# Loads of a two-part activation in the second stage: the low parts issued from ScalarE's queue instead of SyncE's

## The chip, the core and the metric

The kernel is one program on one core of a Trainium2 chip. The metric is the device time of one execution in microseconds (us), the median of several runs. The core's engines are named as in the profile: PE (TensorE matmuls), PEld (its weight loads), DVE (VectorE), ACT (ScalarE), POOL (GpSimd) and SP (SyncE). SPq and ACTq are DMA issues by SP and by ACT.

## The reference, cut to what matters

Three layers run one after the other over 8 batches of 576 tokens: attention with pooled keys and values, a gated MLP with a spatial mixing matrix, and a layer of four small attention experts of which each token takes two. The diff touches only the third, whose input x is the second layer's output:

```python
logits = x @ w_gate                                  # best 2 of 4 experts, softmax weights w
for e in range(4):
    q, k, v = x @ wq[e], x @ wk[e], x @ wv[e]        # x: 576 x 512, head width 64
    scores = causal(0.125 * (q @ k.transpose(0, 2, 1)))
    a = softmax(scores)
    ye = a @ v @ wo[e]
    out += w_e * ye                                  # for tokens that chose e
```

## The kernel before

The program has two stages. The first (class PhaseA) computes the attention and the MLP of all 8 batches, ends near 585 us in the trace, and leaves x in DRAM as two fp32r parts that add up to the fp32 value: a high part and a low part (line 466). The second (class PhaseB) is the expert layer. Each matmul product of it is made of three passes, high by high, low by high and high by low.

**Loading x.** For each batch, load_x is called four times, once for each chunk kc of 128 of the 512 features. Each call issues three DMAs from SP: the high part (line 642, tile xbh, 288 KB), the low part (line 643, into xbl, 288 KB) and a copy of the last 64 tokens of the low part beside the high one (line 644, 32 KB). There is one tile xbl for all four chunks and no second copy: the loads of the next batch wait until the last projection of this batch has read it.

**Units.** A batch is 18 units: two pairs p of experts with 9 units u each. Unit u=0 is the 64 tokens left over of both experts at once, u=1 to 4 are 128 tokens of the first expert with 512, 384, 256 and 128 keys, u=5 to 8 the same of the second. For one unit PE makes the scores (line 839 or 827, tile s), DVE takes the maximum (line 841), ACT the exponential (line 844, tile pr), DVE sum and reciprocal (lines 855, 856), POOL or DVE scales (line 860), PE transposes (line 886 or 873, tile t), and ACT and DVE copy the transposed block as high and low part (lines 890, 891; for u=0 lines 877, 882). The transposes run three units behind the scores (LAG = 3). After u=5 and u=8, PE multiplies by the values (line 906, tile av): ACT and DVE add its two halves (lines 910, 911) and split the sum (lines 916, 917), and the output projection (lines 928 to 931) reads that.

**Filling in.** Between the units stand other pieces of work, by the table FILL: in pair 0 the projections of pair 1 ('12 10 11' and '13', lines 713 to 715, copied by lines 726 to 745), then the loads of the next batch ('x0 x1 x2 x3') straight behind '13', then the output projections of the batch before ('o3 o1 o0'); in pair 1 the value and pair-0 projections of the next batch ('v0', 'v1 00 02', ...). The first batch has its own table without the output projections, the last one loads nothing.

**What sets the order.** Instructions are recorded in the order of the code. When the program is built, a scheduler orders each engine's queue by its own estimate of when operands are there, and each engine then runs its queue strictly in that order. All PSUM tiles of the second stage share eight banks, so a matmul that starts a new tile waits until the readers of the bank's last tile are done. The DMAs of SP and ACT share eight completion counters (DMAHW0 to DMAHW7), which are handed out in turn: an issue waits until the DMA that used its counter eight DMAs ago has landed.

Of the kernel before, what the change touches and what calls it, by code (L numbers as in the profile page):

```python
# [8 lines left out]
F32 = mybir.dt.float32  # L9
# [615 lines left out]
class PhaseB:  # L625
# [8 lines left out]
    def load_x(self, b, kc):  # L634
        nc, w = self.nc, self.w
        if kc == 0:
            self.X[b] = []
            self.xlt = w.tile([128, 4, S], F32R, tag="qt", name="xbl")
        xh = w.tile([128, 640], F32R, tag="P", name="xbh", bufs=5)
        xl = self.xlt[:, kc]  # L640
        d = self.x2d[b][:, kc]
        nc.sync.dma_start(xh[:, :S].bitcast(F32), d[:, 0])
        nc.sync.dma_start(xl.bitcast(F32), d[:, 1])
        nc.sync.dma_start(xh[:, S:].bitcast(F32), d[:, 1, 512:])
        self.X[b].append((xh, xl))

# [369 lines left out]
```

## Time and profile before

| | us |
|---|---|
| runs before: median (lowest to highest) | 962.95 (962.15 to 963.11) |
| the profiled execution | 959.79 |
| its span, first to last instruction | 958.0 |
| PE / DVE / ACT / POOL busy in the span | 909.0 / 688.1 / 518.0 / 445.8 |

The profile is of one execution, whose own time lies 3.2 us under the median of the runs and 1.8 us over its span. The mean granted TensorE clock is 0.983 of full speed.

### The profile page before, as it was taken

The page shows a single profiled execution, that of the slowest core. Times are in us where ns is not written, and L with a number is a line of the kernel's source. Part 1 is how long each engine was busy: PE and PEld are TensorE (multiplying, and loading weights), DVE is VectorE, ACT ScalarE, POOL GpSimd, SP SyncE. Part 2 cuts the span into 40 slices and gives each one's busy share as a digit, 9 for nine tenths or more (in the row PEclk, how much of TensorE's full clock was granted, in tenths as well). Part 3 has the DMA queues.
Part 4 walks back from the last instruction along what each step waited for, and adds up shares of the span by engine and source line. Part 5 has one row for each costly group of instructions (what it writes and reads, how often), then busy time and mean ns, then how long its engine had stood idle before and what let it go on. Part 6 is the DMA issues. An engine that isn't in the chain of part 4 may idle for free.

```text
span 958.0 us, 18445 instructions
## 1 busy us (share of the span) xinstructions
PE 909.0 (95%) x6488; PEld 862.2 (90%) x6488; DVE 688.1 (72%) x1869; ACT 518.0 (54%) x1285; POOL 445.8 (47%) x628
## 2 busy tenths in 40 slices
PE   4887699999999999999999999899999999999997
PEld 3676689989989999899899899799999999999987
DVE  6998458757667577587576524897879797878785
ACT  3765344343443343443443433677777776877776
POOL 6545847558369377475583461122222222323221
PEclk9798899999999999999999999999999999999999
DMA  9611422312402403223116014415353534435121
GB/s 323 244 35 44 162 92 83 122 61 72 160 23 87 156 24 132 99 83 121 62 50 206 13 41 133 141 37 178 79 172 87 160 98 134 133 95 165 49 62 75
DMA packets 51644, 102.86 MB, mean 107 GB/s; under 512 B 10592, under 2 KB 16736, under 8 KB 50656
## 3 DMA queue, kind: packets, MB, share of 16 engines
q1 hardware_dynamic: 51408, 101.68, 33.0%
q8 instruction: 52, 0.85, 0.4%
q14 instruction: 40, 0.33, 0.1%
q10 hardware_dynamic: 144, 0.00, 0.0%
HBM read 59.72 MB, written 28.31 MB: 92 GB/s over the span
## 4 chain that ended last, share of the span: by engine, by line
PE 77%; DVE 11%; ACT 4%; POOL 3%; issue 2%; DMA 2%; SPq 1%; POOLq 0%; ACTq 0%; DVEq 0%
PE av L906 4%; PE op L457 4%; PE op L458 4%; PE op L459 3%; PE sc L224 3%; PE up L416 3%; PE up L418 3%; PE sp L434 3%; PE sp L433 3%; PE sp L432 3%; PE up L417 3%; PE vp L355 3%; PE vp L356 3%; PE vp L357 3%; PE t L886 3%; PE pj L715 2%
## 5 line engine op out<-in xcount | busy, mean ns | idle before, releaser
L860 POOL TENSOR_SCALAR pr<-pr,sm,gw 128x128 f32<-128x128 f32 (+3 forms) x119 | 72.2, 609 | 208.4 <-DVE sm L856 137.6
L844 ACT ACTIVATE pr<-s,sm 128x256 f32<-128x256 f32 (+4 forms) x160 | 83.0, 520 | 41.9 <-DVE sm L841 18.0
L458 PE MATMUL op<-g,woh 128*128 128x288 f32 x256 | 76.9, 301 | 8.0 <-POOL g L445 8.0
L432 PE MATMUL sp<-wsh,vnh 128*128 128x288 f32 x256 | 78.2, 307 | 5.3 <-ACT vnh L400 5.3
L416 PE MATMUL up<-x,wih 128*128 128x288 f32 x256 | 76.9, 300 | 1.6 <-ACT xu L324 1.6
L457 PE MATMUL op<-g,woh 128*128 128x288 f32 x256 | 77.5, 307 | 0.3 <-DVE x2l L464 0.3
L433 PE MATMUL sp<-wsh,vnl 128*128 128x288 f32 x256 | 76.7, 300 | 0.4 <-DVE vnl L402 0.3
L434 PE MATMUL sp<-wsl,vnh 128*128 128x288 f32 x256 | 76.3, 298 | 0.0
L418 PE MATMUL up<-x,wil 128*128 128x288 f32 x256 | 75.8, 296 | 0.0
L715 PE MATMUL pj<-xbh,wql 128*128 128x288 f32 x256 | 75.5, 295 | 0.0
L714 PE MATMUL pj<-xbl,wqh 128*128 128x288 f32 x256 | 75.5, 295 | 0.0
L713 PE MATMUL pj<-xbh,wqh 128*128 128x288 f32 x256 | 75.4, 295 | 0.0
L459 PE MATMUL op<-g,wol 128*128 128x288 f32 x256 | 75.4, 299 | 0.0
L417 PE MATMUL up<-x,wih 128*128 128x288 f32 x256 | 75.1, 293 | 0.0
L841 DVE CUSTOM_DVE_ANT_0 s<-s,mk 128x512 f32<-128x512 f32 (+3 forms) x128 | 62.4, 487 | 3.5 <-PE t L886 2.9
L891 DVE TENSOR_TENSOR pbl<-t,pbh 128x512 fp32r<-128x512 f32 (+3 forms) x128 | 60.7, 484 | 3.3 <-ACT pbh L890 1.7
L886 PE MATMUL t<-ident,pr 128*128 128x128 f32 x320 | 57.7, 280 | 4.8 <-POOL pr L860 2.6
L224 PE MATMUL sc<-kbd,qt 128*128 128x144 f32 (+1 forms) x320 | 49.8, 303 | 11.5 <-DMA qt<-q_in 8.9
L906 PE MATMUL av<-pbh,vt 128*128 128x320 f32 (+4 forms) x224 | 55.7, 278 | 2.4 <-ACT pbh L890 2.4
L400 ACT ACTIVATE vnh<-vg,rs 128x512 fp32r<-128x512 f32 (+1 forms) x40 | 27.3, 718 | 54.9 <-POOL rs L392 43.0
L224 PEld LDWEIGHTS sc<-kbd,qt 128*128 128x128 f32 (+1 forms) x320 | 44.3, 191 | 14.0 <-issue 11.4
L458 PEld LDWEIGHTS op<-g,woh 128*128 128x128 f32 x256 | 48.7, 190 | 8.4 <-POOL g L445 8.2
(247 smaller groups left out, 3305.3 us busy)
## 6 DMA issues: line engine op xcount, KB each, us to landing
kraw<-k_in SPq DMA_DIRECT2D x16, 576.0 KB, 3.8
x<-x2h SPq DMA_DIRECT2D x32, 288.0 KB, 2.1
x<-x2l SPq DMA_DIRECT2D x32, 288.0 KB, 2.1
xbl<-x SPq DMA_DIRECT2D x32, 288.0 KB, 4.0
xbh<-x SPq DMA_DIRECT2D x32, 288.0 KB, 3.8
kd<-scr SPq DMA_DIRECT2D x64, 144.0 KB, 2.5
out<-o SPq DMA_DIRECT2D x32, 288.0 KB, 3.4
vraw<-v_in SPq DMA_DIRECT2D x16, 512.0 KB, 4.2
```

The source lines that it names most:

```text
L224: nc.tensor.matmul(ps[:m, p // 2, (p % 2) * 144:(p % 2) * 144 + 144], qt[:, p, o:o + m], kbd[:, p, :], start=p % 2 == 0, stop=True, skip_g ...
L416: nc.tensor.matmul(o, self.wi[0][:, kc, c], xh, start=kc == 0, stop=False)
L417: nc.tensor.matmul(o, self.wi[0][:, kc, c], xl, start=False, stop=False)
L418: self.upmm = nc.tensor.matmul(o, self.wi[1][:, kc, c], xh, start=False, stop=kc == 3).ins
L432: nc.tensor.matmul(o, vh[:, k, c], self.ws[0][:, k, s], start=k == 0, stop=False)
L433: nc.tensor.matmul(o, vl[:, k, c], self.ws[0][:, k, s], start=False, stop=False)
L434: nc.tensor.matmul(o, vh[:, k, c], self.ws[1][:, k, s], start=False, stop=False)
L457: nc.tensor.matmul(o, self.wo[0][:, k, c], gh[:, s], start=k == 0, stop=False)
L458: nc.tensor.matmul(o, self.wo[0][:, k, c], gl[:, s], start=False, stop=False)
L459: nc.tensor.matmul(o, self.wo[1][:, k, c], gh[:, s], start=False, stop=k == 3)
L715: nc.tensor.matmul(ps, self.wq[1][:, kc, c], xh[:, s], start=False, stop=kc == 3)
L906: nc.tensor.matmul(ps[:, s - lo:], vt[:, j, 2 * p + e].rearrange("p a d -> p (a d)"), t[:, e, j * PTS + s:j * PTS + up], start=j == 0 and ...
```

## The change

The 32 loads of the low parts (four for each batch) are issued by ACT; the 64 others of load_x stay on SP. Tiles, sizes, and the arithmetic are as they were.

```diff
@@ PhaseB.load_x
         nc.sync.dma_start(xh[:, :S].bitcast(F32), d[:, 0])
-        nc.sync.dma_start(xl.bitcast(F32), d[:, 1])
+        nc.scalar.dma_start(xl.bitcast(F32), d[:, 1])
         nc.sync.dma_start(xh[:, S:].bitcast(F32), d[:, 1, 512:])
```

Since the scheduler orders all queues anew, the order moves on other engines too. Two places follow, both in the third batch of the second stage, in pair 0, just behind the projection '13'. The loads there are those of the fourth batch (x_3).

ACT's queue before, from the last copies of the q projection (734) to the exponential of unit 4 (844, 128x128):

```order
L734 ACTIVATE qs_6011<-pj 64x64
L744 ACTIVATE scr<-pj 128x288 [waits PE_49]
L844 ACTIVATE pr,sm<-s,sm 128x256 [waits DVE_49]
L910 ACTIVATE scr<-av 64x256 [waits PE_49]
L916 ACTIVATE ah<-scr 128x256 [waits DVE_49]
L910 ACTIVATE scr<-av 64x320 [waits PE_49]
L877 ACTIVATE pbh<-t_7743 128x4x2x64 [waits PE_49,Activation_49]
L877 ACTIVATE pbh<-t_7750 64x2x64 [waits PE_49]
L916 ACTIVATE ah<-scr 128x320 [waits DVE_49]
L844 ACTIVATE pr,sm<-s,sm 128x128 [waits DVE_49]
```

and ACT's queue after, over the same stretch (the names in brackets are the counters waited for):

```order
L734 ACTIVATE qs_6011<-pj 64x64
L643 DMA xbl<-x_3_60 128x576 [waits DMAHW1_49,DMAHW0_49,PE_49]
L844 ACTIVATE pr,sm<-s,sm 128x256 [waits DVE_49]
L744 ACTIVATE scr<-pj 128x288 [waits PE_49]
L643 DMA xbl<-x_3_60 128x576
L643 DMA xbl<-x_3_60 128x576 [waits DMAHW6_49]
L643 DMA xbl<-x_3_60 128x576 [waits DMAHW0_49]
L910 ACTIVATE scr<-av 64x256 [waits PE_49]
L910 ACTIVATE scr<-av 64x320 [waits PE_49]
L877 ACTIVATE pbh<-t_7743 128x4x2x64 [waits PE_49,Activation_49]
L877 ACTIVATE pbh<-t_7750 64x2x64 [waits PE_49]
L844 ACTIVATE pr,sm<-s,sm 128x128 [waits DVE_49]
```

The four issues stand in it, three of them in a row ahead of the first copy of av (910), the last one waits for counter 0 (the one of the high-part load of chunk 1, which SP issues a little earlier), and both 916 have moved behind the exponential of unit 4.

DVE's queue before, from the first sum of av's halves (911) to the maximum of unit 5 (841, 128x512):

```order
L911 TENSOR_TENSOR scr<-av,scr 64x256
L917 TENSOR_TENSOR al<-scr,ah 128x256
L911 TENSOR_TENSOR scr<-av,scr 64x320
L841 ISA s,sm<-s,mk 128x128
L841 ISA sm 128x1
L882 TENSOR_TENSOR pbl<-t_7743,pbh 128x4x2x64
L917 TENSOR_TENSOR al<-scr,ah 128x320
L882 TENSOR_TENSOR pbh<-t_7750,pbh 64x2x64
L891 TENSOR_TENSOR pbl<-t,pbh 128x4x128
L841 ISA s,sm<-s,mk 128x512
```

and DVE's queue after:

```order
L745 TENSOR_TENSOR qs_6011<-pj,scr 128x288
L841 ISA s,sm<-s,mk 128x128
L841 ISA sm 128x1
L841 ISA s,sm<-s,mk 128x512
L841 ISA sm 128x1
L911 TENSOR_TENSOR scr<-av,scr 64x256
L911 TENSOR_TENSOR scr<-av,scr 64x320
L882 TENSOR_TENSOR pbl<-t_7743,pbh 128x4x2x64
L917 TENSOR_TENSOR al<-scr,ah 128x256
L917 TENSOR_TENSOR al<-scr,ah 128x320
```

The maxima of units 4 and 5 (841, 128x128 and 128x512) have moved ahead of the two sums 911. On PE the order here stays as it was up to the output projection: scores of unit 5, transposes of unit 2, scores of unit 6 (839, 128x384), then 928; only a few matmuls of 928 to 930 change places among themselves. In both programs the scores of unit 6 take the bank of av's first half and wait for 911 64x256.

The same two pictures stand in six batches, the second to the seventh. In the first batch the three issues stand ahead of the copies 877 instead (there is no output projection), and the eighth loads nothing.

## Rows read from the trace of the kernel before

**Rows 1.** Page, part 1: busy us, share of the span, instructions.
```profile
PE 909.0 (95%) x6488; PEld 862.2 (90%) x6488; DVE 688.1 (72%) x1869; ACT 518.0 (54%) x1285; POOL 445.8 (47%) x628
```

**Rows 2.** Windows: length, busy us by engine, granted clock, DMA share, GB/s.
```profile
600.00:650.00 50.00, 45.43 (x332) 43.14 (x331) 43.03 (x176) 34.34 (x110) 9.57 (x16) 0.97 0.37 102
650.00:800.00 150.00, 149.49 (x1156) 146.71 (x1155) 120.69 (x483) 112.49 (x355) 40.38 (x64) 1.00 0.44 132
```

**Rows 3.** Timeline of PE: start, us, instruction, [idle before <- releaser].
```profile
651.34 0.42 PE L839 MATMUL s<-kd,qs 128*128 128x384 f32 x1
...
695.76 0.39 PE L840 MATMUL s<-qs,qzvlo 128*128 128x512 f32 x1
...
696.24 0.42 PE L839 MATMUL s<-kd,qs 128*128 128x384 f32 x1
696.49 0.34 PE L840 MATMUL s<-qs,qzvlo 128*128 128x384 f32 x1
696.67 0.28 PE L928 MATMUL op<-ah,wqh 128*128 128x256 f32 x1
...
876.28 0.42 PE L839 MATMUL s<-kd,qs 128*128 128x384 f32 x1
```

**Rows 4.** Timeline of DVE, third batch of the second stage.
```profile
694.53 0.42 DVE L911 TENSOR_TENSOR scr<-av,scr 64x256 f32<-64x256 f32 x1
...
695.89 0.48 DVE L911 TENSOR_TENSOR scr<-av,scr 64x320 f32<-64x320 f32 x1
696.30 0.28 DVE L841 CUSTOM_DVE_ANT_0 s<-s,mk 128x128 f32<-128x128 f32 x1
...
698.64 0.69 DVE L841 CUSTOM_DVE_ANT_0 s<-s,mk 128x512 f32<-128x512 f32 x1
```

**Rows 5.** Timeline of ACT, the same place.
```profile
692.48 0.45 ACT L734 ACTIVATE qs<-pj 64x64 fp32r<-64x64 f32 x2 [0.36 <-DVE qs L731]
692.95 0.41 ACT L744 ACTIVATE scr<-pj 128x288 fp32r<-128x288 f32 x1
693.53 0.47 ACT L844 ACTIVATE pr<-s,sm 128x256 f32<-128x256 f32 x1 [0.17 <-DVE sm L855]
...
694.12 0.38 ACT L910 ACTIVATE scr<-av 64x256 f32<-64x256 f32 x1
...
696.79 0.35 ACT L844 ACTIVATE pr<-s,sm 128x128 f32<-128x128 f32 x1
```

**Rows 6.** All issues of line 643: ns min/median/max, and us from issue to landing.
```profile
L643 SPq DMA_DIRECT2D xbl<-x x32: 325/430/1244, 503.3 to 879.0; - x32
...
DMA to landing us min/median/max: 2.9/4.0/5.5
```

**Rows 7.** The only DMA issued by ACT (line 83).
```profile
L83 ACTq DMA_DIRECT2D cm<-cm_in x1: 409/409/409, 0.7 to 0.7; - x1
```

**Rows 8.** Timeline of SP: at the program's start, and in the third batch.
```profile
0.74 0.86 SPq L58 DMA_DIRECT2D kraw<-k_in  x2
...
691.64 0.54 SPq L642 DMA_DIRECT2D xbh<-x  x1
```

**Rows 9.** Timeline of PE, ACT: first batch of the second stage.
```profile
604.97 0.75 ACT L877 ACTIVATE pbh<-t 128x512 fp32r<-128x512 f32 x2
...
612.18 1.09 PE L886 MATMUL t<-ident,pr 128*128 128x128 f32 x4 [1.45 <-DVE sm L855]
```

**Rows 10.** Windows, columns as in Rows 2: first batch, last batch.
```profile
611.00:612.00 1.00, 0.00 (x0) 0.00 (x0) 1.00 (x6) 0.77 (x3) 0.00 (x0) 0.95 0.97 321
612.00:613.00 1.00, 0.82 (x5) 0.85 (x5) 0.79 (x8) 0.23 (x2) 0.43 (x1) 0.50 1.03 336
...
614.00:615.00 1.00, 1.00 (x7) 1.00 (x6) 0.88 (x2) 0.25 (x2) 0.00 (x0) 0.50 0.78 275
...
945.00:949.00 4.00, 3.13 (x23) 2.88 (x23) 2.62 (x8) 2.21 (x7) 0.00 (x0) 1.00 0.07 24
```

**Rows 11.** Timeline of ACT at the last scores of the first stage.
```profile
505.03 0.69 ACT L245 ACTIVATE e<-e 64x576 f32<-64x576 f32 x1 [1.37 <-DVE e L237]
```

## The prediction, written before the changed kernel was run

> **What bounds the kernel now.** Read first the page's busy shares [rows 1]: PE is busy 95% of the span, no other engine above 72%. Such a share is a mean, so the windows come next. In the second stage's steady part PE is busy 149.49 of 150 us at full clock, ACT 112.5 and DVE 120.7; only around the first batch, from 600 to 650 us, is PE idle for 4.6 us [rows 2]. So from the second batch on whatever makes PE wait is paid in full, there is next to nothing for earlier loads to win (0.5 us in 150), and a wait that is inserted once per batch counts as often as it stands. Last comes the timeline of each engine at the place where the loads stand. I walk the third batch: PE runs the scores of unit 5 to 696.15 (695.76 + 0.39), starts those of unit 6 (128x384) at 696.24 and the output projection at 696.67 with no idle time before any of these; the unit-6 scores stand at 651.34 in the first of six alike batches and at 876.28 in the last [rows 3].
>
> **The change part by part.**
>
> *What SP loses.* Four issues of 0.43 us per batch [rows 6], 1.7 us of a queue that PE does not wait for. Gain: none, by the 0.5 us just read; bound at 0.5 us.
>
> *What ACT gets.* The same 32 issues. I price one at 0.43 us; the one DMA that ACT issues today took 0.41 [rows 7]. In total 32 x 0.43 = 13.8 us on an engine that idles 37.5 us in 150 [rows 2]. The mean would hide it; the place decides. Walk ACT's new queue on the old clock [rows 5]: the copies of line 734 end at 692.93; the first 643 runs to 693.4 and fits into the 0.17 us of idle time and the slot that 744 had; the exponential of unit 3 goes from 693.53 to 694.1; 744 (0.41) to 694.5. Three issues follow. The last one also waits for its counter, that is for the high part of chunk 1 to land, issued at 691.64 [rows 8]; with 4.0 us for a load of this size [rows 6] that is 695.64, about when it comes up anyway (694.5 + 2 x 0.43 = 695.4). It ends at 696.1. Then 910 (0.38) to 696.5 instead of 694.5, the second 910 to 696.9, the two 877 to 697.6, and the exponential of unit 4 with its readout to 698.1, where it began at 696.79.
>
> *What DVE's new order does.* The maxima of units 4 and 5 now precede both sums 911. The maximum of unit 5 cannot begin before PE has ended that unit's scores at 696.15, and it holds DVE about 0.7 us [rows 3, 4]. So 911 64x256 starts near 696.9 and ends near 697.3; before it ran from 694.53 to 694.95 [rows 4]. In both programs PE's scores of unit 6 wait for just this sum, since they take its bank: they start at about 697.35 instead of 696.24, 1.1 us late. This does not hang on what a DMA issue costs on ACT: its copy 910 is done at 696.5, 0.4 us before DVE is free for the sum.
>
> *What is late next.* After the unit-6 scores PE would reach the output projection at about 697.8 (0.43 us behind, as in 696.24 to 696.67). Its first bank is now the one of unit 4's scores, freed by ACT's exponential at 698.1. So it starts 1.4 us late (698.1 against 696.67). Behind it nothing gives time back: PE waits for nothing later in the batch, so it carries the 1.4 us on. The copies 916 and splits 917 come about when PE asks for them; I count nothing for them.
>
> *Bounds per batch.* Below, 1.1 us: issues on ACT cost nothing and only DVE's order counts. Above: the landing takes its maximum of 5.5 us [rows 6], the last issue begins at 697.1 instead of 695.64, and the projection starts 2.9 us late. I take 1.4, because 4.0 is the median and ACT's own 0.41 is the nearest row to its issue.
>
> *The first batch.* Same four issues, other table: they stand ahead of the two 877 (604.97 before [rows 9]), which go about 2.4 us later (one issue and 744 ahead of them more or less in free time, the rest not). PE is starved there anyway, so part is absorbed: between 0 and 2.4, I take 1.0, since the wait that ends the starved stretch (1.45 us for DVE [rows 9]) is at the end of the same chain.
>
> *The four loads of the first batch,* issued in the first stage: ACT idles 1.37 us before its next exponential there [rows 11], so two issues (0.86) are hidden and the others stand in front of a copy with idle time around it. Nothing; at most 0.9 us once if the cover were gone.
>
> *Other queues.* The counters tie SP to ACT: the third kd copy of pair 1's keys now waits for ACT's first load to land (about 697). Keys are needed only when pair 1 begins, behind all output projections; nothing, but up to 1.5 us per batch if landings stretch to 5.5. Loads of chunk 3 come no later than before, since SP has fewer issues ahead of them.
>
> *Sum.* 6 x 1.4 + 1.0 = 9.4 us. On the profiled execution that makes 959.79 + 9.4 = 969.2; its time lies 3.2 below the median of the runs, on which it makes 962.95 + 9.4 = **972.3 us**, 1.0% slower.
>
> **A rule weighed against this.** The rows first: ACT's one issue took 0.41 us at 0.7 us, while SP issued two in 0.86 [rows 7, 8], so one pair in which both queues issue at once shows no surcharge. The Trainium skill, page "Perfetto Trace Analysis", section "DMA Instruction — HWDGE (DVE, Sync)", says that descriptors are generated by a block that the issuing sequencers share, that an issue locks it for exclusive use, and that the time spent waiting for the lock is inside the profiled duration. By that rule ACT's issues lengthen whenever SP issues beside them, and the sum is that of the first rival. The trace does not agree in the one pair that it has, which is a small transfer.
>
> **The rivals.**
>
> *Issues on ACT are dearer than on SP.* If each of the three in a row takes 0.86 us because SP issues its key copies at the same time, they end at 697.1 (694.5 + 3 x 0.86) instead of 696.1, and all behind them is 1.0 us later: 6 x 2.4 + 2 = 16.4, 979.4 us. For: the median issue is 0.43, but one took 1.24 [rows 6]. Against: rows 7.
>
> *The stalls bring the clock down.* In the first batch PE stood still for the whole of 611 to 612 after a starved stretch, and the granted clock was 0.50, the 1.2 GHz level, from 612 to 615 [rows 10]. If each of the six stalls did that, three us at half rate cost 1.5 each: 9 more, 981 us. Against: from 945 to 949 PE was idle 0.87 of 4 us and the clock stayed at 1.00, the 2.4 GHz level [rows 10].
>
> *Nothing to measure.* DVE or PE have slack that the walk misses, and ACT's 37.5 idle us take the issues: within 2 us, 963. For: the busy means. Against: the unit-6 scores have no idle time before them and a wait for a sum that stands behind unit 5's maximum. A halfway case, stalls of 0.5 us, gives 966.
>
> *Faster.* In the first batch the maxima now run ahead of the copies of finished blocks, so probabilities could be ready sooner and the starved stretch shrink, with its half clock: at most 4.6 us of idle time [rows 2] and 1.5 of clock, 6.1 together. It decides only if the six stalls together stay under that, below 1.0 us each, which the order speaks against: 960 at best, with stalls of 0.5.
>
> **How the numbers follow.** Forecast case, 1.1 to 2.0 us per batch and 0 to 2 in the first (969 to 977): 0.63. Dearer issues: 0.15. Clock: 0.05. Halfway: 0.07. Nothing: 0.06. Faster: 0.04. A change under 0.2% (1.9 us) can't be told from none here. So slower 0.90, same 0.06, faster 0.04. The range leaves out the two last cases and part of the clock case and of the dearer issues: 965.5 to 981.
>
> **What the profile after would show.** Right: PE's list of waits gains one of about 1.1 us, six times, at line 839 for DVE's line 911, and a smaller one at the first 928 for ACT; PE's busy time unchanged at 909; batches 1.4 us longer than their 44.9 (651.34 to 876.28 is five of them [rows 3]); 32 issues on ACT of about 0.43 us; clock 1.00 in the steady part. Wrong: ACT issues of 0.8 us or more, or waits of ACT for landings above 1 us; no wait at 839; a clock of 0.50 behind the stalls; or waits of PE for x or kd loads, which I count at nothing.

## The result, and the profile after

The kernel after takes 972.84 us, the median of four runs from 970.74 to 973.33; the kernel before takes 962.67 (four runs, 962.15 to 963.11). The ratio is 1.0107, with a 95% interval from 1.0093 to 1.0120: slower by 10.2 us, where 9.4 were forecast. The profiled execution of after took 970.74 us with a span of 969.0, that of before 959.79 with 958.0.

The busy times on the page, with the same columns as [rows 1]:

```profile
PE 913.1 (94%) x6488; PEld 864.3 (89%) x6488; DVE 691.0 (71%) x1869; ACT 519.4 (54%) x1285; POOL 446.8 (46%) x628
```

The span is 11.0 us longer. PE's busy time, which the prediction took for unchanged, is 4.2 us of that by the windows of the trace: 2.1 in the first stage, 0.7 in the first batch of the second (at a lower clock, below) and 1.4 in the batches behind it. The other 6.8 us are idle time, and the list of PE's waits from 625 us to 958 us, which leaves the first batch of the second stage out, says where most of it stands. Columns: who waited <- for what, us in total, times, longest:

```profile
PE s L839 <- DVE scr L911: 6.5, 6, 1.1
PE av L906 <- ACT pbh L890: 2.4, 3, 1.0
PE av L906 <- DVE pbl L891: 1.2, 5, 0.4
PE t L886 <- POOL pr L860: 0.7, 1, 0.7
```

The first row is new: six waits, one for each batch from the second to the seventh, each of the scores of unit 6 for DVE's sum. The other three stand in before's list too, with 2.4, 1.4 and 0.7. PE's timeline shows one place of the first batch and the batches' waits; compare the last three places with [rows 3]:

```profile
612.19 0.33 PE L886 MATMUL t<-ident,pr 128*128 128x128 f32 x1 [2.28 <-POOL pr L860]
...
613.15 1.09 PE L886 MATMUL t<-ident,pr 128*128 128x128 f32 x4 [0.45 <-DVE sm L856]
615.17 0.61 PE L827 MATMUL s<-kd,qs 128*128 128x320 f32 x1 [0.93 <-DMA xbh<-x]
616.40 0.61 PE L828 MATMUL s<-kd,qs 128*128 128x320 f32 x1 [0.63 <-DMA kd<-scr]
...
655.82 0.44 PE L839 MATMUL s<-kd,qs 128*128 128x384 f32 x1 [1.08 <-DVE scr L911]
...
700.36 0.40 PE L840 MATMUL s<-qs,qzvlo 128*128 128x512 f32 x1
...
702.16 0.44 PE L839 MATMUL s<-kd,qs 128*128 128x384 f32 x1 [1.08 <-DVE scr L911]
...
702.62 0.28 PE L928 MATMUL op<-ah,wqh 128*128 128x256 f32 x1
...
887.16 0.44 PE L839 MATMUL s<-kd,qs 128*128 128x384 f32 x1 [1.08 <-DVE scr L911]
```

From the last scores of unit 5 to the first of unit 6 it is 1.80 us (702.16 - 700.36); before it was 0.48 (696.24 - 695.76). Of these 1.32 us more, 1.08 are listed as idle; the rest is the modelled end of the transposes between them, which now stand alone in front of the gap. From 655.82 to 887.16 are five batches: 231.34 us against 224.94 [rows 3], 1.28 more for each.

DVE and ACT at the same place, the third batch; the columns are those of [rows 4, 5]. DVE:

```profile
699.97 0.30 DVE L841 CUSTOM_DVE_ANT_0 s<-s,mk 128x128 f32<-128x128 f32 x1 [0.49 <-PE s L840]
...
700.90 0.70 DVE L841 CUSTOM_DVE_ANT_0 s<-s,mk 128x512 f32<-128x512 f32 x1 [0.57 <-PE s L840]
701.52 0.14 DVE L841 DVE_READ_ACCUMULATOR2_ANT sm<- 128x1 f32 x1
701.69 0.82 DVE L911 TENSOR_TENSOR scr<-av,scr 64x256 f32<-64x256 f32 x2
```

ACT:

```profile
697.16 0.33 ACTq L643 DMA_DIRECT2D xbl<-x  x1
...
698.12 0.48 ACT L844 ACTIVATE pr<-s,sm 128x256 f32<-128x256 f32 x1 [0.60 <-DVE sm L855]
698.13 0.33 ACTq L643 DMA_DIRECT2D xbl<-x  x1
...
698.50 0.44 ACTq L643 DMA_DIRECT2D xbl<-x  x1
698.59 0.40 ACT L744 ACTIVATE scr<-pj 128x288 fp32r<-128x288 f32 x1
699.26 0.33 ACTq L643 DMA_DIRECT2D xbl<-x  x1
699.64 0.70 ACT L910 ACTIVATE scr<-av 64x256 f32<-64x256 f32 x2 [0.65 <-PE t L873]
...
701.02 0.35 ACT L844 ACTIVATE pr<-s,sm 128x128 f32<-128x128 f32 x1
```

DVE idles 0.57 us for PE's scores of unit 5, takes their maximum, and only then adds the halves of av. The first of ACT's two copies, which the sum needs, took 0.38 us in [rows 5], so here it was done near 700.0, 1.7 us before the sum began. So it is DVE's place in its queue, not ACT, that PE waits for.

All issues of line 643 (ns min/median/max) and their time to landing, to set beside [rows 6]:

```profile
L643 ACTq DMA_DIRECT2D xbl<-x x32: 326/327/728, 503.8 to 884.4; - x32
...
DMA to landing us min/median/max: 2.8/5.7/9.1
```

An issue is cheaper than it was on SP (median 0.33 us against 0.43), a landing takes longer (5.7 us against 4.0).

The rest of the loss is in the first batch. Two windows hold it, from 0.64 us ahead of the stage's first 128x384 scores to the same matmul of the second batch; columns as in [rows 2]. Before:

```profile
599.19:642.06 42.87, 38.35 (x279) 36.35 (x278) 36.25 (x148) 28.96 (x95) 7.26 (x12) 0.96 0.35 99
```

After, with two slices of it:

```profile
599.83:645.14 45.31, 39.09 (x279) 36.63 (x278) 36.67 (x148) 29.12 (x95) 7.30 (x12) 0.92 0.35 94
...
613.00:614.00 1.00, 0.85 (x4) 0.72 (x4) 0.69 (x6) 0.00 (x0) 0.72 (x2) 0.50 0.83 197
...
618.00:619.00 1.00, 1.00 (x6) 1.00 (x6) 0.97 (x6) 0.00 (x0) 0.00 (x0) 0.50 0.00 0
```

It is 2.4 us longer: 1.7 more of idle time (6.22 against 4.52) and 0.7 more of busy time for the same 279 matmuls, at the granted clock of 0.50 that lasts from about 612.8 to 619.5 here and ended within 615 to 616 before. So the balance of the two profiled executions is: 0.6 us at the stage's start (600.47 against 599.83 for its first 128x384 scores), 2.4 in the first batch, and 7.9 in the six batches behind it (323.86 - 315.94 us from that matmul to the end of the span); together 10.9 of 11.0. The 0.6 us is no part of the change: in the executions profiled for this study the second stage began 0.1 us earlier to 3.1 us later than in before's, and by 2.6 us in e3 below, whose loads in the first stage are those of before.

### The profile page after: what moved, and what is told of

Same layout as the page of the kernel before. It is cut to its first block, busy times and chain, and to the rows that moved or that the text cites. A ratio compares the mean times of both kernels' runs of the same rounds, so it can differ in the third digit from the quotient of the medians.

```text
span 969.0 us, 18452 instructions
## 1 busy us (share of the span) xinstructions
PE 913.1 (94%) x6488; PEld 864.3 (89%) x6488; DVE 691.0 (71%) x1869; ACT 519.4 (54%) x1285; POOL 446.8 (46%) x628
## 4 chain that ended last, share of the span: by engine, by line
PE 79%; DVE 9%; ACT 4%; POOL 3%; DMA 2%; issue 2%; SPq 0%; POOLq 0%; ACTq 0%; DVEq 0%
PE av L906 4%; PE sc L224 4%; PE op L457 4%; PE op L458 4%; PE op L459 3%; PE up L416 3%; PE up L418 3%; PE up L417 3%; PE sp L434 3%; PE sp L433 3%; PE sp L432 3%; PE vp L355 3%; PE vp L356 3%; PE vp L357 3%; PE pj L713 3%; PE pj L715 3%
## 5 line engine op out<-in xcount | busy, mean ns | idle before, releaser
L224 PEld LDWEIGHTS sc<-kbd,qt 128*128 128x128 f32 (+1 forms) x320 | 44.7, 193 | 15.3 <-issue 10.9
L839 PE MATMUL s<-kd,qs 128*128 128x512 f32 (+3 forms) x128 | 50.0, 391 | 6.5 <-DVE scr L911 6.5
```

Source lines behind the costliest of these rows:

```text
L224: nc.tensor.matmul(ps[:m, p // 2, (p % 2) * 144:(p % 2) * 144 + 144], qt[:, p, o:o + m], kbd[:, p, :], start=p % 2 == 0, stop=True, skip_g ...
```

## The experiments

**Theory A** is that of the prediction: DVE's order, with unit 5's maximum ahead of the sum, is the whole steady cost. The rivals: **B**, the issues cost by themselves, by the time and the waits that they put into ACT's queue; and **C**, which e1 brought up, the large transfers of a second queue come in the way of the key copies kd and of each other. Each expectation says with its numbers what it holds of which. Every kernel was run beside the kernel before on the same chip; the medians of before were 961.8 to 962.3, and "more" or "less" below is against the one of the same series.

**Which batches pay.** The loads of two batches, or of the six others, on ACT:

```diff
-        nc.scalar.dma_start(xl.bitcast(F32), d[:, 1])
+        (nc.scalar if b >= 2 else nc.sync).dma_start(xl.bitcast(F32), d[:, 1])   # e3
+        (nc.scalar if b < 2 else nc.sync).dma_start(xl.bitcast(F32), d[:, 1])    # e4
```

> The low parts of the first two batches are loaded from SP again, those of the third to the eighth batch from ACT. If the two places add up (six stalls of 1.3 us in batches two to seven, and 2.4 us in the first batch of the stage): 962.7 + 7.9 = about 970.5 us, and the first batch looks like that of the kernel before. If instead the first batch carries most of the 10 us through its half clock: about 965.

> The counterpart: only the low parts of the first two batches are loaded from ACT, the others from SP. If the places add up: 962.7 + 2.4 to 3.1 (the first batch, and up to 0.6 in the first stage) = 965 to 966 us, with a wait of about 2.3 us for POOL's scaling of unit 4 and no wait at line 839. If the first batch carries most: about 970.

Measured: e3 969.46 us, ratio 1.0074 [1.0061, 1.0087], 7.7 us more; e4 964.32, 1.0018 [1.0006, 1.0031], 2.5 more. The two add up to 10.2, the cost of the change. In e3 PE's waits from 625 us on have the row of after unaltered, and its first batch is as long as before's (45.42 us between the first 128x384 scores of the two batches, 45.31 before, 47.75 after; that 45.31 is also the length of after's window above is chance):

```profile
PE s L839 <- DVE scr L911: 6.5, 6, 1.1
```

So the steady waits cost 7.7 us and the first batch, with the loads issued in the first stage, 2.5.

**The order alone undone.** The kernel after, with DVE's maximum of unit 5 tied behind the first sum; the loads stay on ACT:

```diff
-            nc.vector.tensor_tensor_reduce(o, o, self.mk[...], ...)
+            with self.tc.issue_after(self.sum[b - 1, 1, 1, 0]) if b and not p and u == 5 else nullcontext(): nc.vector.tensor_tensor_reduce(o, o, self.mk[...], ...)
...
-        nc.vector.tensor_add(a[64 * e:64 * e + 64, lo:up], ps[:64], bt)
+        self.sum[b, p, e, g] = nc.vector.tensor_add(a[64 * e:64 * e + 64, lo:up], ps[:64], bt).ins
```

> All 32 low-part loads stay on ACT, at the same place of its queue ahead of 910; only DVE's maximum of unit 5 (841, 128x512) is made to stand behind the first sum 911 in batches two to seven. Theory A (DVE's order costs the steady part): the six waits of 1.1 us at line 839 for line 911 go, and with them 6 x 1.3 us: 972.8 - 7.9 = about 965. Theory B (ACT's issues make its copies 910 late, and the sums with them, whatever DVE's order): the waits at 839 stay, now for 911 behind a late 910, and the time stays at 972 to 973.

Measured: 970.13 us, ratio 1.0091 [1.0072, 1.0109]. Five of the six waits are gone, yet the time is not. PE's waits from 625 us on:

```profile
PE s L828 <- DMA kd<-scr: 2.6, 2, 2.1
...
PE s L839 <- DVE scr L911: 0.6, 1, 0.6
PE s L827 <- DMA xbh<-x: 0.5, 1, 0.5
```

PE's timeline at the longest of the new ones, and the clock behind it:

```profile
801.37 0.46 PE L828 MATMUL s<-kd,qs 128*128 128x320 f32 x1 [2.11 <-DMA kd<-scr]
```

```profile
802.00:804.00 2.00, 2.00 (x11) 2.00 (x10) 1.07 (x6) 0.00 (x0) 0.00 (x0) 0.50 0.58 222
```

Here PE waits for keys: with the loads on a second queue a copy of keys took up to 9.0 us to land over the whole run (median 2.5), where before none took over 4.0. In after it was up to 8.6 too, but from 625 us on PE's list holds no wait for it. So A is right about the waits and wrong that they are all there is to remove: the stall of 1.1 us per batch covered a second loss, which comes into view when the stall goes. That is C. It is uneven: the five batch lengths between e1's first and last scores of unit 6 are 0.3 to 3.7 us above before's. Not all of it is C: about 0.23 us in each of the six batches stand at the output projection (the part on fewer loads says how that is seen).

**The order alone made.** The kernel before, all loads on SP, with the copies and sums of av, and the copies of unit 1's transposes, recorded behind unit 5's scores and the sum tied behind its maximum (the last of several edits is shown):

```diff
-        nc.vector.tensor_add(a[64 * e:64 * e + 64, lo:up], ps[:64], bt)
+        with self.tc.issue_after(self.mx) if late else nullcontext(): nc.vector.tensor_add(a[64 * e:64 * e + 64, lo:up], ps[:64], bt)
```

> All loads stay on SP as in the kernel before; only the copies and sums of av (910, 911, 916, 917) and the copies of unit 1's transposes are recorded behind the scores of unit 5 in batches two to seven, so that DVE's maxima of units 4 and 5 stand ahead of both sums 911, as in the changed kernel. Theory A: six waits of 1.1 to 1.4 us at line 839, 962.7 + 7.9 = about 970.5 us. Theory B: no DMA is issued by ACT, its 910 is early, and the time stays within 2 us of 962.7.

Measured: 964.13 us, ratio 1.0022 [1.0012, 1.0031]. The time that A gave was missed, but this tells little of A, since something else moved with the order: the unit-6 scores no longer take the bank that the sum frees (in the third batch they start at 698.70, the sum at 699.83). PE's waits have instead

```profile
PE op L928 <- DVE scr L911: 1.2, 6, 0.2
```

So the late sum is not harmless here, only cheaper: a matmul of the output projection waits for it. From the first to the twelfth matmul of the projection it is 1.92 us in each of the six batches, 1.45 to 1.47 in before: 0.47 more, and six times that is 2.8 us against the 2.3 measured. More than half of it is in no list of waits (the part on fewer loads says why).

**Away from the projection.** The kernel after with the loads moved behind the output projections, so that DVE's order at unit 5 is before's again:

```diff
-FILL = (('', '12 10 11', '', '13 x0 x1 x2 x3', '', '', 'o3 o1 o0', '', ''), ...
+FILL = (('', '12 10 11', '', '13', '', '', 'o3 o1 o0 x0 x1 x2 x3', '', ''), ...
```

> All 32 low-part loads are on ACT, but the loads of batches three to eight are recorded three units later (behind 'o3 o1 o0'): in ACT's queue only one issue is left ahead of 910, and DVE's sums 911 stand ahead of the maxima again. Theory A (DVE's order costs the steady part, the queue and the issue time as such cost nothing): no wait at 839, the steady part of the kernel before, the first batch of the changed kernel (+2.5 us): 965 us. Theory C (transfers on a second queue delay the keys and other loads, wherever they are issued): waits for kd or x as in the run with the sum first, 968 to 970 us.

Measured: 967.33 us, ratio 1.0056 [1.0040, 1.0072]. No wait at line 839 is left; the first batch, whose table is unchanged, costs what it did in after (47.73 us). That leaves some 3 us in the others: the time lies between the two expectations and meets neither. PE's list from 625 us on has only one new entry of weight, 0.7 us in three waits for xbl. Most of the rest stands at the output projection, here in the third batch:

```profile
703.42 0.47 ACT L916 ACTIVATE ah<-scr 128x320 fp32r<-128x320 f32 x1
...
703.55 0.28 PE L929 MATMUL op<-ah,wql 128*128 128x256 f32 x1
703.67 0.28 PE L930 MATMUL op<-al,wqh 128*128 128x256 f32 x1
703.98 0.38 PE L928 MATMUL op<-ah,wqh 128*128 128x320 f32 x1
```

ACT makes the second half of ah 1.04 us behind the start of the unit-6 scores (702.38), where before it was 0.17 (696.41 against 696.24), and PE starts the matmul that reads it 0.31 us behind the one ahead, not 0.12. In each of the six batches the projection starts 0.15 us later behind these scores than in before, and its first twelve matmuls take 1.81 us instead of 1.45: 0.5 us per batch, 3.0 in all.

**Small transfers on ACT.** The kernel before with 64 of 576 columns of each low part on ACT and 512 on SP, four issues per batch as in after:

```diff
+        nc.scalar.dma_start(xl[:, :64].bitcast(F32), d[:, 1, :64]); nc.sync.dma_start(xl[:, 64:].bitcast(F32), d[:, 1, 64:])
```

> ACT issues as many loads at the same place ahead of 910, but each of only the first 64 columns of the low part (32 KB); SP loads the other 512 columns. DVE's sums stand ahead of the maxima, much as in the run with the sum first. Theory C (in that run what was left of the cost were keys that landed late, since 288 KB loads of a second queue moved beside them): the kd landings go back to 4 us at most, PE waits for no kd, and what stays is the first batch and some tenths per batch: 965 to 967 us. Rival (what was left there comes from the four issues on ACT and the order behind them): 969 to 970 us as in that run.

Measured: 963.07 us, ratio 1.0011 [0.9998, 1.0023]: not to be told from no change, and less than was expected, since the first batch costs nothing either. Copies of keys land within 4.1 us again, and the first batch is 45.22 us long, although its first copy 877 starts as late as in after (7.06 us behind the first 128x384 scores; 7.08 in after, 5.14 in before).

To compare the two orders of DVE with small transfers, ACT got seven issues of 32 columns (one of chunk 3, two of each other), which turns the order as in after; e10 is e9 with the tie of e1:

```diff
+        [nc.scalar.dma_start(xl[:, c:c + 32].bitcast(F32), d[:, 1, c:c + 32]) for c in ((0, 32) if kc < 3 else (0,))]; c = 64 if kc < 3 else 32; nc.sync.dma_start(xl[:, c:].bitcast(F32), d[:, 1, c:])
```

> Hardly any bytes move to ACT's queue: ACT issues seven loads of 32 columns (16 KB) per batch, SP the rest of the low parts. Seven issues instead of four, so that DVE's order is that of the changed kernel: maxima of units 4 and 5 ahead of both sums, PE's unit-6 scores waiting for the sum. Theory A (DVE's order by itself costs the steady part): six waits of 1.1 us or a little more at line 839, no wait for kd, first batch near that of the kernel before: 961.8 + 1.2 + 7.9 = about 970 to 971 us. Theory C (it takes large transfers on ACT's queue): 963 to 965 us.

> The same seven small issues at the same place ahead of 910, but DVE's maximum of unit 5 held behind the first sum. Theory A: the waits at 839 go, 963 to 964 us, 7 us under its twin. Theory B (ACT's issue time makes 910 and the sums late): waits at 839 of 0.5 us and more stay, 966 us or above. Theory C: the same time as its twin.

Measured: e9 983.98 us, ratio 1.0229 [1.0198, 1.0260]; e10 979.05, 1.0171 [1.0153, 1.0190]. Both are far above what was expected. The twins differ by 4.9 us, but this is not the order's price, since the waits that it was to remove stay. ACT's timeline in e9:

```profile
702.34 2.93 ACTq L643 DMA_DIRECT2D xbl<-x  x4
705.31 0.70 ACT L910 ACTIVATE scr<-av 64x256 f32<-64x256 f32 x2 [2.83 <-DMA xbl<-x]
```

ACT's list of waits in e9 from 625 us on:

```profile
ACT scr L910 <- DMA xbl<-x: 18.2, 6, 3.5
```

Four issues in a row took 2.93 us, because with eight counters and this many DMAs an issue waits for an earlier one to land, and the copies 910 stand behind them: 3.0 us in each of six batches. PE's six waits for line 911 are 9.2 us in e9 and, for the copies' sake though the sum stands first, 9.4 in e10; e9 has six more at line 928 for ACT's late exponential (844), 2.3 us. So B is true where counters run short: such an issue holds its engine until an earlier transfer has landed, not for its own 0.33 us. In after's third batch that is 0.32 us at most: the issues there took 0.33 to 0.44 us, and the last began 0.32 us behind the end of the one ahead.

**Fewer loads on ACT.** Two and three of the four loads of a batch:

```diff
+        (nc.scalar if kc in (2, 3) else nc.sync).dma_start(xl.bitcast(F32), d[:, 1])      # e11
+        (nc.scalar if kc in (1, 2, 3) else nc.sync).dma_start(xl.bitcast(F32), d[:, 1])   # e12
```

> Only the low parts of chunks 2 and 3 are loaded from ACT (16 issues, 288 KB each), those of chunks 0 and 1 from SP; DVE's sums stand ahead of the maxima without an edge of mine. If large transfers on ACT's queue delay the keys in proportion to their bytes: half of what the run with the sum first lost, 964 to 966 us, kd landings above 4 us in some batches. If only DVE's order counts: 962 to 963.5 us.

> Three of the four low parts are loaded from ACT; the sums still stand ahead of the maxima, so that only the fourth load turns DVE's order round. If DVE's order is the whole steady cost: no wait at 839 above 0.5 us, 963 to 964 us. If late keys take its place as in the run with the sum first: waits for kd and their half clock, 966 to 968 us. If neither matters but the issue count: three quarters of 10 us, 970 us, with the waits at 839.

Measured: e11 961.75 us, ratio 0.9997 [0.9988, 1.0007]; e12 963.75, 1.0016 [1.0006, 1.0025]. The expectation by which the order is the whole steady cost was met. With 24 of the 32 loads on ACT the cost is 1.8 us, with all 32 it is 10.2. PE's timeline in e12, in the first batch and in the third:

```profile
613.76 0.33 PE L886 MATMUL t<-ident,pr 128*128 128x128 f32 x1 [2.29 <-POOL pr L860]
...
614.71 1.09 PE L886 MATMUL t<-ident,pr 128*128 128x128 f32 x4 [0.45 <-DVE sm L856]
615.45 0.61 PE L827 MATMUL s<-kd,qs 128*128 128x320 f32 x1
615.86 0.47 PE L828 MATMUL s<-kd,qs 128*128 128x320 f32 x1
...
698.44 0.49 PE L886 MATMUL t<-ident,pr 128*128 128x128 f32 x3
698.69 0.44 PE L839 MATMUL s<-kd,qs 128*128 128x384 f32 x1
```

and DVE's in the third batch:

```profile
697.83 0.30 DVE L841 CUSTOM_DVE_ANT_0 s<-s,mk 128x128 f32<-128x128 f32 x1 [0.49 <-POOL pr L860]
...
698.22 0.82 DVE L911 TENSOR_TENSOR scr<-av,scr 64x256 f32<-64x256 f32 x2
```

Three loads on ACT leave the sum ahead of unit 5's maximum, and the unit-6 scores start with no idle time; the fourth load turns the order round.

The 1.8 us of e12 stand in the steady part, and in no list of waits. A matmul of 128x256 is drawn 0.28 us long, but the next can start 0.12 us behind it (703.55 and 703.67 in e5's rows), so that a wait of up to 0.16 us leaves no gap. Start to start shows it; e12's third batch again:

```profile
699.67 0.42 DVE L917 TENSOR_TENSOR al<-scr,ah 128x256 fp32r<-128x256 f32 x1
...
699.90 0.38 PE L928 MATMUL op<-ah,wqh 128*128 128x320 f32 x1
700.14 0.38 PE L930 MATMUL op<-al,wqh 128*128 128x256 f32 x1
```

The product with al (930) starts when the first of DVE's two splits 917 is done (700.09), which here stands behind a copy (882). The first twelve matmuls of the projection take 1.81 us in each of the six batches, 0.36 more than in before (2.2 in all); in e1 it is 1.68, in e11 1.44 and in after 1.45. So DVE's order costs something in e12 too, at another place.

The first batch is the other thing to see in e12. Its 2.29 us for POOL are those of after (2.28), and so are the 0.45 behind them. But then the key scores (827, 828) follow at once, where after waits 0.93 and 0.63 us for DMAs. In e12 a copy of keys in that stretch (600 to 625 us) took 6.3 us to land at the median, in after 8.0, in before 3.2; and e12's first batch is 45.01 us long. C is borne out: what the first batch costs in after is late transfers, not the copies 877. A later ACT can cost the first batch as well: in e9, where issues hold it, the first 877 starts 9.55 us behind the scores, PE waits 1.7 us for ACT's exponential, and the batch takes 47.43 us although its copies of keys land within 3.3 us.

**Reordering the first batch, and a better version.** In before, ACT's exponential of unit 5 ahead of its copy of unit 3's transposes in the first batch (e7); and the same together with e5's table and loads on ACT from the third batch on (e8):

```diff
-            nc.scalar.activation(d(ph), v, AF.Copy)
+            with self.tc.issue_after(self.ex[0, 0, 5]) if (b, p, u) == (0, 0, 3) else nullcontext(): nc.scalar.activation(d(ph), v, AF.Copy)
```

> The kernel before with one change of order: in the first batch ACT's exponential of unit 5 (844, 128x512) goes ahead of the copy of unit 3's transposes (890, 128x256), for which ACT idled 0.9 us. If the starved stretch at 611 us hangs on that exponential: it starts 0.9 us sooner, PE's wait of 1.45 us for DVE falls to about 0.5 and with it some half clock, 1 to 2.5 us faster, about 961. If another chain ends there at the same time, or the half clock comes all the same: no change.

> Low parts of batches three to eight on ACT and recorded three units later as in the run with later loads, those of the first two batches on SP, and the order of the run with the exponential first. If these places are independent: the steady part of the kernel before, its first batch less 1 to 2.5 us, 960 to 962 us. If ACT's later issues cost the steady part something after all: above 963.

Measured: e7 961.99 us, ratio 1.0000 [0.9990, 1.0010]; e8 964.11, 1.0024 [1.0012, 1.0037]. In e7's profile the first batch is 0.5 us shorter (44.83), too little for the timing to show, where one wait of 1.5 us went and one of 0.9 for DVE's scaling came. e8 missed its hope of a gain too: its projection has e5's half microsecond in each of the six batches (1.81 us for the twelve matmuls, and the start 0.15 us later). No kernel of the study is faster than the one before.

## Why the prediction was right, step by step

**SP gains nothing.** No run separates this term. Nothing contradicts it: e11 takes half of the low parts' issues off SP, adds no wait at line 839, and measures 0.9997.

**What ACT gets.** The walk was too pessimistic here: 0.33 us for most issues, not 0.43, and it set issues and ACT's computing one behind the other, where the issues at 698.13 and 698.50 ran beside 844 and 744. On the old clock (4.53 us earlier, by the first 839 of the third batch, 694.49 against 689.96) the first 910 ran from 695.1, not from 696.1. It changed nothing, as the prediction itself said it would not: the sum waits for DVE's own place.

**DVE's new order.** Right in kind, place and nearly in size. The sum was forecast for 696.9 and the scores of unit 6 for 697.35, 1.1 us late. On the old clock they came at 697.16 and 697.63. The first is 0.26 later than forecast mostly because the walk started unit 5's maximum at 696.15, where it ran from 696.37, and left out its readout, which ends 0.06 us behind it (rows of DVE above).

**What is late next.** The result was right, the reason was not. The projection was forecast at 698.1 for a bank that ACT frees; it came at 698.09 on the old clock, but without any wait of its own. It is 0.46 us behind the scores (702.62 - 702.16), as before (0.43), and its first twelve matmuls take 1.45 us as before. ACT's exponential of unit 4, at 701.02 with its row of 0.35 us and a readout, was done a microsecond ahead. All the lateness is that of line 839, and that the sum of this term came out is luck. Waits of the projection for this exponential do show in e9, where issues hold ACT: six, 2.3 us together.

**The price per batch.** 1.4 was taken, 1.31 measured (7.9 over six). This term is 7.9 where 8.4 was forecast. (The batch of before, by its own five, is 45.0 us, not 44.9: 224.94 / 5.)

**The first batch.** This is the term that was mis-sized: 1.0 taken, 2.4 measured in the profile (2.5 in e4's time), the top of its range of 0 to 2.4. Its mechanism failed too, so that the size lies in the range is luck. The prediction let the copies 877 come late, and they do, by 1.9 us; but in e6 they are as late, e12 and e6 have the waits for POOL that this makes (2.29 and 2.7 us at the longest), and their first batches cost nothing, 45.01 and 45.22 us against 45.31. What after has and these lack is PE's waits for loads and keys (0.93 and 0.63 us), which the prediction counted at nothing and named as a sign of being wrong, and the half clock that goes on through those waits.

**Counters and landings counted as nothing.** Half right. In after PE waits for no load or key from the second batch on, as said. But e1 shows that this rests on the stall: with it gone, keys land too late in places. The bound of 1.5 us per batch covers that: e1 as a whole costs 8.3 us, of which its first batch is 2.2 by its 47.46 us, the projection 1.4 and the one wait left at line 839 0.6, so late transfers and the clock behind them are left some 4 us, 0.7 per batch. They were not an addition to the 1.4 but stood in its shadow.

**The rivals.** Dearer issues: not so, median 0.327 and at most 0.728 us. The Trainium skill, page "Perfetto Trace Analysis", section "DMA Instruction — HWDGE (DVE, Sync)", puts the wait for a shared descriptor generator into the profiled duration of an issue. The trace of e6 agrees. Where an issue of ACT starts within 0.02 us behind one of SP's key issues, as it does in five batches of e6 and in five of e9, it takes 0.68 to 0.70 us, twice the 0.33:

```profile
651.35 0.59 SPq L751 DMA_DIRECT2D kd<-scr  x1
...
651.37 0.68 ACTq L643 DMA_DIRECT2D xbl<-x  x1
```

So the rival's surcharge is real, 0.35 us for one issue. In after it was not met: its issues that begin inside one of SP's begin later in it, most of them 0.2 to 0.45 us behind its start, and took 0.33. Clock: not at 1.1 us, since from 650 to 800 us after has the level of 2.4 GHz throughout (granted clock 1.00, mean over 625 to 969 us with all six waits in it: 1.00). But e1's 2.11 us brought 0.50. Nothing, halfway and faster: out, by six waits and the interval.

**What stays open.** The order with no other loss beside it was never built: e2 changed a bank, e9 and e10 hit the counters. So that it costs 1.31 us per batch is shown in after, but not that removing it would return 7.9 us; e1 says it would not as long as the transfers are there. Why the landings stretch is not settled: no run tells the second queue from the mere number of large loads in flight with the keys (in before's third batch two loads are issued ahead of the four key copies and the others behind them, in after six large loads before the second of them). Nor is it settled why e1's losses differ so from batch to batch.

## What to carry to other kernels

Where a scheduler orders the queues, look at what a moved issue does to the order of the other engines before pricing the issue itself: here 0.33 us on ACT was free, and one maximum ahead of one sum on DVE cost 1.3 us per batch. Beside the list of waits, compare the starts of the same matmuls: 0.2 to 0.5 us per batch stood in no list. A stall hides what arrives late behind it, so removing it is not worth its length until the next latest operand has been priced. And move loads in portions: three of four cost 1.8 us, the fourth 8.4.

## What the runs showed of the hardware

With 288 KB loads on a second queue the other queue's copies took longer: keys (144 KB, line 751) from at most 4.0 us to at most 8.6, and the loads themselves from a median of 4.0 to 5.7; with 64 of 576 columns on it the keys stayed at 4.1. An issue on ACT can run beside ACT's own computing (698.13 beside the exponential of 698.12). It took 0.33 us, and 0.68 where it started with one of SP's. Late counters can hold a compute engine far longer than the issues themselves: 2.93 us for four (e9). The clock stayed at 1.00 behind six waits of 1.08 us in a PE that was otherwise busy and behind one of 1.97 in e9, and fell to 0.50 behind one of 2.11 in e1 and, in e10, behind one of 2.46.
